# Attention and gated feed-forward on one core: softmax weights normalised on GpSimd before their transposes, and the weights' check moved into their decoding

## The chip, the cores and the metric

The kernel runs on one core of a Trainium2 chip. Its engines are TensorE (PE), VectorE (DVE), ScalarE (ACT), GpSimd (POOL) and the queue of SyncE (SP) that issues loads. The metric is the device time of one execution in microseconds; less is better.

## The reference

Banded causal attention with 8 global keys feeds a gated feed-forward block. B = 4, H = 8, S = 768, D = 64, d_model = 512, d_ff = 1024.

```python
scores = q @ k.T / sqrt(D) + bias            # bias: -slope * distance
keep   = (key < n_global) | ((rel >= 0) & (rel < n_local))     # 8 and 96
a = exp(where(keep, scores, -1e9) - max)
a = a / (a.sum(-1) + 1e-9)
x = a @ v                                    # heads side by side: B, S, 512
h = relu(x @ w_in)                           # B, S, 1024
c = conv over the sequence, 3 taps, per channel
out = (h * sigmoid(c)) @ w_out
```

The three feed-forward weights come as 64-bit floats.

## The kernel before

**Attention.** A job m is one batch, one half of the sequence (384 queries) and one pair of heads: 4 x 2 x 4 = 32 jobs. Each job has three steps of 128 queries, so there are 96 steps s. A step needs only 232 keys (136 in the first block of a sequence): 96 before, 128 own, 8 global. The parts of a step, by function:
- `scores`: TensorE, two heads into one PSUM tile `s` (two of these).
- `maxima`: VectorE adds the bias table and takes the row's least (`mm`).
- `exps`: ScalarE writes the exponentials to `pbuf[s % 3]` and their row sums to `sums`.
- `transposes`, LAG_T = 2 steps later: four TensorE transposes into PSUM `t`, copied by ScalarE to a tile `pt` (three of these).
- `values`, after a job's last step and LAG_V = 3 steps behind: PV, 24 matmuls into the one PSUM tile `pv`.

The exponentials go through the transposes and PV unnormalised. The inverse sums take a way of their own: `inverses` (VectorE, a sum and a reciprocal of 6 columns per job), `spread` (GpSimd copies them 64 times side by side into `wide`), `turned` (three TensorE transposes into `rt`, ScalarE copy to `rs`). `mixed` multiplies `pv` by `rs` on VectorE, GpSimd rounds it to `xh`, and VectorE leaves the rest in `xl`; products with high and low halves keep the precision.

**Feed-forward.** Four jobs make a unit of 384 rows, and there are 8 units. `mm1` (tile `h`, 96 matmuls a unit) and `relu`; `conv` (GpSimd takes the first tap, VectorE two more); `gate` (tanh on ScalarE); `split` (VectorE and ScalarE); `mm2` (tile `o`, 24 matmuls for each of 24 blocks of rows). This work is queued and `fill` puts it between the steps.

**Weights.** Sixteen pieces of 0.5 MB (`wr`) are decoded: three bit operations on VectorE (`weight_bits`), a cast on GpSimd (`weight_high`) and a subtraction on VectorE (`weight_low`). They are chores that `work` hands out from step 1 on with a budget per step. The fast path holds only for words of moderate size, so `check_weights` loads all 16 pieces again at the end (`check`) and VectorE takes each piece's smallest square, ScalarE the sum of squares. What is found goes into `bad`; one matmul (`total`) sums it over the partitions, and the flag decides whether the exact path `general` runs. With these inputs it does not.

**Order.** Steps 0 to 10 stand in the order in which the code is written (`manual_schedule`). From step 11 a scheduler with its own model of the engines sets the order on each engine; at run time each engine takes its instructions in that order and waits where an operand is missing.

Of the kernel before, what the change touches and what calls it, by code (L numbers as in the profile page):

```python
# [34 lines left out]
LAG_T, LAG_V = 2, 3  # L35
# [27 lines left out]
def fast_path(tc, io):  # L63
# [89 lines left out]
    reli = p2.tile([P, NT], I32, tag="pt", name="reli", bufs=NB)  # L153
# [14 lines left out]
    keyi = p2.tile([P, 64], I32, tag="pt", name="keyi", bufs=NB)  # L168
# [44 lines left out]
    misc = const.tile([P, 2 * NCHK + NLOW + 12], F32, name="misc")  # L213
# [3 lines left out]
    bad, ones, ebias, gbias = (rest[:, k : k + 1] for k in range(8, 12))  # L217
    G.memset(gbias, -0.96)

# [86 lines left out]
    words = []  # L306

    def check_loads(n):
        while len(words) < n:
            k = len(words)  # L310
            X = p1 if k % 3 == 2 else p2
            t = X.tile([P, HW, 2], I32, tag="rk" if k % 3 == 2 else "kk", name=f"check{k}")
            nc.sync.dma_start(t, weight_words(*divmod(k, 2)))
            words.append(t[:, :, 1].bitcast(F32))

    def check_weights():
        for k in range(NCHK):
            check_loads(k + 1)
            x = words[k]
            junk = p2.tile([P, HW], F32, tag="qh", name=f"junk{k}")  # L320
            j2 = p2.tile([P, HW], F32, tag="ql", name=f"junkb{k}")
            V.tensor_tensor_reduce(
                out=junk, in0=x, in1=x, scale=-1.0, scalar=-3.0e38,
                op0=ALU.mult, op1=ALU.max, accum_out=chk[:, k : k + 1],
            )
            A.activation(j2, x, AF.Square, accum_out=chk[:, NCHK + k : NCHK + k + 1])
        small, large = chk[:, :NCHK], chk[:, NCHK:]
        V.tensor_scalar(small, small, -1.5 * 2.0**-30, None, ALU.is_gt)
# [13 lines left out]
    st_s, st_pt, pv, xt, sums, rs, wides = {}, {}, {}, {}, {}, {}, {}  # L342
# [32 lines left out]
    def maxima(s):  # L375
        m, i = steps[s]
        b, u, hp = jobs[m]
        sp, c0, n, first = st_s[s]
        mm = p1.tile([P, 2], F32, tag="mm", name=f"mm{s}", bufs=6)
        if i == 0:  # L380
            sums[m] = p1.tile([P, 3, NB, 2], F32, tag="sums", name=f"sums{m}", bufs=3)
        for j in range(2):
            h = 2 * hp + j
            tb = tab[:, h, WIN:] if first else tab[:, h, 0:WIN]
            last_ttr[s] = V.tensor_tensor_reduce(  # L385
                out=sp[j][:, c0 : c0 + n], in0=sp[j][:, c0 : c0 + n], in1=tb,
                scale=-0.125, scalar=3.0e38, op0=ALU.add, op1=ALU.min,
                accum_out=mm[:, j : j + 1],
            )
        st_s[s] = (sp, c0, n, mm)  # L390

    def exps(s):
        m, i = steps[s]
        sp, c0, n, mm = st_s[s]
        pb = pbuf[s % NPB]
        for j in range(2):
            last_exp[s] = A.activation(  # L397
                pb[:, j, c0 : c0 + n], sp[j][:, c0 : c0 + n], AF.Exp,
                bias=mm[:, j : j + 1], scale=-1.0, accum_out=sums[m][:, 0, i, j : j + 1],
            )  # L400
        st_s[s] = (pb, c0)

    def inverses(m):
        su, more, inv = (sums[m][:, k] for k in range(3))
        V.tensor_scalar(more, su, 1.0e-9, None, ALU.add)
        V.reciprocal(inv, more)

    def spread(m):
        inv = sums.pop(m)[:, 2]
        wide = p2.tile([P, NB, 2, D], F32, tag="wide", name=f"wide{m}", bufs=1)  # L410
        G.tensor_copy(wide, inv.unsqueeze(3).broadcast_to([P, NB, 2, D]))
        wides[m] = wide.rearrange("p i j d -> p i (j d)")

    def turned(m):
        wide = wides.pop(m)
        pt = ps_t.tile([P, 2, 2, P], F32, tag="t", name=f"rt{m}")
        flat = pt.rearrange("p j c q -> p (j c q)")[:, :TB]
        for i in range(NB):
            T.transpose(flat[:, i * P : (i + 1) * P], wide[:, i], ident)  # L419
        rs[m] = p2.tile([P, TB], F32, tag="rs", name=f"rs{m}", bufs=1)  # L420
        A.activation(rs[m], flat, AF.Copy)

    def transposes(s):
        m, i = steps[s]
        pb, c0 = st_s.pop(s)
# [5 lines left out]
        sb = p2.tile([P, 2, 2, P], F32, tag="pt", name=f"pt{s}", bufs=NB)  # L431
# [7 lines left out]
    def values(m):  # L439
        pv[m] = ps_v.tile([P, TB], F32, tag="v", name=f"pv{m}")  # L440
        for i in range(NB):
            sb, ka = st_pt.pop(NB * m + i)
            for c, n in ((0, ka), (1, P - 24)):
                for j in range(2):
                    T.matmul(  # L445
                        pv[m][64 * j : 64 * j + 64, i * P : (i + 1) * P],
                        vt[m][:n, i, c, 64 * j : 64 * j + 64],
                        sb[:n, j, c, :],
                        start=c == 0,
                        stop=c == 1,  # L450
                    )

    def mixed(m):
        xh = px.tile([P, TB], F32R, tag="xh", name=f"xh{m}")
        xl = px.tile([P, TB], F32R, tag="xl", name=f"xl{m}")
        xt[m] = (xh, xl)
        x = rs.pop(m)
        V.tensor_tensor(x, pv[m], x, ALU.mult)  # L458
        G.tensor_copy(xh, x)  # L459
        cur["mixed"] = V.tensor_tensor(xl, x, xh.bitcast(F32), ALU.subtract)  # L460
# [215 lines left out]
    chores = {"dve": [], "pool": []}  # L676
# [12 lines left out]
    def piece_bits(i, half, n):  # L689
        weight_bits(i, half, n)  # L690
        if n == 2:
            chores["pool"].append((cur["s"], 0.7, piece_high, (i, half)))
            free_slot((i, half))
# [30 lines left out]
    for s in range(len(steps) + LAG_V + 1):  # L724
        cur["s"] = s
        m, i = steps[s] if s < len(steps) else (len(jobs), -1)
        if s < HAND:
            scores(s)
            if ends(s - LAG_V):
                values((s - LAG_V) // NB)  # L730
                turned((s - LAG_V) // NB)
            if s >= LAG_T:
                transposes(s - LAG_T)
            maxima(s)
# [20 lines left out]
            work("pool", 1.3)  # L755
        else:
            if hand:
                hand = False
                manual.__exit__(None, None, None)
# [15 lines left out]
            if s <= len(steps) and i < 1:  # L775
                inverses((s - 1) // NB)
                spread((s - 1) // NB)
# [4 lines left out]
            if ends(s - LAG_V):  # L782
                values((s - LAG_V) // NB)
                turned((s - LAG_V) // NB)
# [203 lines left out]
```

## Time and profile before

| | |
|---|---|
| median of 3 runs | 495.19 us (494.72 to 497.38) |
| the profiled execution | 490.68 us, span 488.8 us |
| busy in the span | TensorE 462.9 us, VectorE 364.7, ScalarE 287.3, GpSimd 164.9 |
| granted TensorE clock | mean 0.966 |

The profiled execution took 4.51 us less than the median of the runs, so a sum made against the profile is carried over to the runs as a difference. A busy TensorE is no proof that it bounds: its ends are modelled and overlap. The chain of waits and the idle time ahead of an instruction say more.

### The profile page before, as it was taken

Reading aid. Unit: us, or ns where it says so; the run is one execution under the profiler, and the core shown is the slowest. Engines: PE = TensorE matmul, PEld = TensorE weight load, DVE = VectorE, ACT = ScalarE, POOL = GpSimd, SP = SyncE. Lnnn points to the kernel's source line nnn. Section 1 sums busy time; section 2 is a strip of 40 time slices with the busy share of each in tenths; the row PEclk is TensorE's granted clock in tenths of the full one; section 3 lists DMA queues with packets and bytes.
Section 4 is the critical chain, followed back from the end, with each engine's and each line's share of the span. In section 5 each row is a group of like instructions: output and inputs, shape, how many; then the busy total and the mean of one; then the engine's idle time right before and its main releaser. Section 6 shows DMA issues by size and latency. Waiting matters only on the chain.

```text
span 488.8 us, 8824 instructions
## 1 busy us (share of the span) xinstructions
PE 462.9 (95%) x3109; PEld 398.1 (81%) x3109; DVE 364.7 (75%) x872; ACT 287.3 (59%) x774; POOL 164.9 (34%) x222
## 2 busy tenths in 40 slices
PE   7978999969999999999999999999999999999980
PEld 6855788759988998889888988899989988898860
DVE  4798879979999886857797887758797866167332
ACT  2543546667577585646785567557775774255542
POOL 4333344642553643323542542233434410020000
PEclk8898699998999999999999999999999999999996
DMA  7888662223332522343344323423342312100793
GB/s 191 217 210 255 200 174 89 78 91 107 92 113 98 163 68 87 121 142 108 108 129 130 101 66 115 138 87 101 127 129 96 100 57 84 44 0 23 252 302 119
DMA packets 21364, 60.01 MB, mean 123 GB/s; under 512 B 2880, under 2 KB 3136, under 8 KB 21312
## 3 DMA queue, kind: packets, MB, share of 16 engines
q1 hardware_dynamic: 17856, 53.21, 35.8%
q10 hardware_dynamic: 3456, 6.16, 3.4%
q8 instruction: 26, 0.43, 0.4%
q14 instruction: 26, 0.21, 0.1%
HBM read 53.07 MB, written 6.29 MB: 121 GB/s over the span
## 4 chain that ended last, share of the span: by engine, by line
PE 74%; DVE 14%; DMA 6%; issue 2%; ACT 2%; POOL 0%; SPq 0%; DVEq 0%; ACTq 0%; POOLq 0%
PE h L478 24%; PE o L589 21%; PE pv L445 9%; PE s L366 5%; DMA check<-in_w 5%; PE s L356 4%; PE t L429 4%; PE t L430 3%; PE rt L419 3%; DVE s L385 2%; DVE gl L580 1%; DVE c L577 1%; DVE c L526 1%; DVE c L525 1%; DMA rq<-in_qk 1%
## 5 line engine op out<-in xcount | busy, mean ns | idle before, releaser
L397 ACT ACTIVATE pbuf<-s,mm 128x232 f32<-128x232 f32 (+1 forms) x192 | 82.8, 437 | 73.8 <-DVE mm L385 71.9
L385 DVE CUSTOM_DVE_ANT_0 s<-s,tab 128x232 f32<-128x232 f32 (+1 forms) x192 | 73.8, 385 | 48.8 <-PE s L366 36.3
L524 POOL TENSOR_SCALAR c<-hbuf,cw 128x382 f32<-128x382 f32 (+1 forms) x64 | 47.3, 742 | 96.2 <-ACT hbuf L488 91.0
L589 PE MATMUL o<-woh,gh 128*128 128x512 f32 x192 | 78.5, 409 | 0.0
L589 PE MATMUL o<-wol,gh 128*128 128x512 f32 x192 | 76.2, 397 | 0.0
L589 PE MATMUL o<-woh,gl 128*128 128x512 f32 x192 | 76.1, 397 | 0.0
L445 PE MATMUL pv<-pt,v 104*64 104x128 f32 (+2 forms) x768 | 58.2, 289 | 4.0 <-DVE rs L458 2.9
L478 PE MATMUL h<-xh,wih 128*128 128x384 f32 x252 | 59.9, 348 | 0.0
L445 PEld LDWEIGHTS pv<-pt,v 104*64 104x64 f32 (+2 forms) x768 | 43.3, 141 | 19.6 <-issue 8.9
L525 DVE SCALAR_TENSOR_TENSOR c<-hbuf,cw,c 128x382 f32<-128x382 f32 (+1 forms) x64 | 44.9, 712 | 18.9 <-POOL c L524 18.8
L478 PE MATMUL h<-xl,wih 128*128 128x384 f32 x252 | 58.5, 346 | 0.1
L436 ACT ACTIVATE pt<-t 128x512 f32<-128x512 f32 x80 | 47.1, 599 | 18.5 <-PE t L430 18.2
L478 PE MATMUL h<-xh,wil 128*128 128x384 f32 x252 | 55.8, 342 | 0.0
L429 PE MATMUL t<-ident,pbuf 128*128 128x128 f32 (+1 forms) x192 | 48.9, 281 | 2.6 <-ACT pbuf L397 1.2
L488 ACT ACTIVATE hbuf<-h 128x384 f32<-128x384 f32 x64 | 31.2, 492 | 33.1 <-PE h L478 27.8
L430 PE MATMUL t<-ident,pbuf 128*128 128x128 f32 x192 | 48.3, 278 | 0.0
L459 POOL CAST xh<-rs 128x384 fp32r<-128x384 f32 x32 | 23.8, 743 | 65.6 <-DVE rs L458 65.4
L478 PEld LDWEIGHTS h<-xl,wih 128*128 128x128 f32 x252 | 43.5, 189 | 1.8 <-issue 1.5
L478 PEld LDWEIGHTS h<-xh,wil 128*128 128x128 f32 x252 | 44.3, 188 | 0.8 <-issue 0.8
L526 DVE SCALAR_TENSOR_TENSOR c<-hbuf,cw,c 128x382 f32<-128x382 f32 (+1 forms) x64 | 44.0, 701 | 0.8
L478 PEld LDWEIGHTS h<-xh,wih 128*128 128x128 f32 x252 | 43.5, 189 | 1.1 <-issue 0.8
L589 PEld LDWEIGHTS o<-woh,gl 128*128 128x128 f32 x192 | 36.1, 188 | 8.3
(110 smaller groups left out, 896.5 us busy)
## 6 DMA issues: line engine op xcount, KB each, us to landing
v<-in_vv SPq DMA_DIRECT2D x32, 384.0 KB, 3.1
rq<-in_qk SPq DMA_DIRECT2D x23, 384.0 KB, 3.3
wr<-in_w SPq DMA_DIRECT2D x16, 512.0 KB, 5.3
check<-in_w SPq DMA_DIRECT2D x16, 512.0 KB, 4.8
rk<-in_qk SPq DMA_DIRECT2D x12, 504.0 KB, 3.6
out<-ob ACTq DMA_DIRECT2D x23, 256.0 KB, 3.0
rk<-in_qk SPq DMA_DIRECT2D x11, 408.0 KB, 3.1
rq<-in_qk SPq DMA_DIRECT2D x9, 192.0 KB, 5.7
```

What stands on the lines that cost most here:

```text
L385: last_ttr[s] = V.tensor_tensor_reduce(out=sp[j][:, c0 : c0 + n], in0=sp[j][:, c0 : c0 + n], in1=tb, scale=-0.125, scalar=3.0e38, op0=ALU. ...
L397: last_exp[s] = A.activation(pb[:, j, c0 : c0 + n], sp[j][:, c0 : c0 + n], AF.Exp, bias=mm[:, j : j + 1], scale=-1.0, accum_out=sums[m][:, ...
L429: T.transpose(pt[:ka, j, 0, :], pb[:, j, c0:P], ident)
L430: T.transpose(pt[:, j, 1, :], pb[:, j, P:256], ident)
L436: last_ev[s] = A.activation(sb, pt, AF.Copy)
L445: T.matmul(pv[m][64 * j : 64 * j + 64, i * P : (i + 1) * P], vt[m][:n, i, c, 64 * j : 64 * j + 64], sb[:n, j, c, :], start=c == 0, stop=c ...
L478: T.matmul(ps[:, :TB], w_[:, k, fs], x_, start=part == 0 and k == 0, stop=part == 2 and k == NK - 1,)
L488: A.activation(half, ps[:, :TB], AF.Relu, scale=0.5)
L524: G.tensor_scalar(c, *tap(1), 1.0, ALU.mult, ALU.mult)
L525: V.scalar_tensor_tensor(c, *tap(0), c, ALU.mult, ALU.add)
L526: V.scalar_tensor_tensor(c, *tap(2), c, ALU.mult, ALU.add)
L589: T.matmul(ps, g_[:, f], w_[:, f], start=f == 0 and part == 0, stop=f == NF - 1 and part == 2,)
```

## The change

- `inverses` becomes `normalise`, once a step instead of once a job: VectorE adds 1e-9 to two sums and takes two reciprocals, and GpSimd multiplies the exponentials in `pbuf` by them in place, one instruction per head. It comes one step after `exps` and one before `transposes`. `spread`, `turned`, `wide`, `rt` and `rs` are gone.
- `mixed` is a ScalarE copy of `pv` to `xh` and a VectorE subtraction from `pv`.
- LAG_V is 4, there are four `pt` tiles, and the 24 PV matmuls of a job stand together, the last block first.
- The second load of the weights is gone. As a piece is decoded, ScalarE squares its words and sums them, then takes a relu of those squares with a bias and sums again: two instructions a piece, handed out as chores of their own (`act`), one in a step by hand. Both keep to one tile with the tag `ob`. The last five small VectorE operations of the check stay.

```diff
-LAG_T, LAG_V = 2, 3
+LAG_T, LAG_V = 2, 4
...
-    def check_weights():
-        for k in range(NCHK):
-            check_loads(k + 1)
-            x = words[k]
...
-            V.tensor_tensor_reduce(
-                out=junk, in0=x, in1=x, scale=-1.0, scalar=-3.0e38,
-                op0=ALU.mult, op1=ALU.max, accum_out=chk[:, k : k + 1],
-            )
-            A.activation(j2, x, AF.Square, accum_out=chk[:, NCHK + k : NCHK + k + 1])
+    def piece_check(i, half, n):
+        k = 2 * i + half
+        if n == 0:
+            squares[k] = p1.tile([P, HW], F32, tag="ob", name=f"square{k}")
+            x = wraw[i, half][:, :, 1].bitcast(F32)
+            A.activation(squares[k], x, AF.Square, accum_out=chk[:, NCHK + k : NCHK + k + 1])
+        else:
+            y = squares[k]
+            A.activation(
+                y, y, AF.Relu, bias=least, scale=-(2.0**30), accum_out=chk[:, k : k + 1]
+            )
...
-    def inverses(m):
-        su, more, inv = (sums[m][:, k] for k in range(3))
-        V.tensor_scalar(more, su, 1.0e-9, None, ALU.add)
-        V.reciprocal(inv, more)
...
-        G.tensor_copy(wide, inv.unsqueeze(3).broadcast_to([P, NB, 2, D]))
...
-        for i in range(NB):
-            T.transpose(flat[:, i * P : (i + 1) * P], wide[:, i], ident)
-        rs[m] = p2.tile([P, TB], F32, tag="rs", name=f"rs{m}", bufs=1)
-        A.activation(rs[m], flat, AF.Copy)
+    def normalise(s):
+        pb, c0, n, mm = st_s[s]
+        V.tensor_scalar(mm[:, 4:6], mm[:, 2:4], 1.0e-9, None, ALU.add)
+        V.reciprocal(mm[:, 6:8], mm[:, 4:6])
+        for j in range(2):
+            x = pb[:, j, c0 : c0 + n]
+            G.tensor_scalar(x, x, mm[:, 6 + j : 7 + j], 1.0, ALU.mult, ALU.mult)
...
     def values(m):
         pv[m] = ps_v.tile([P, TB], F32, tag="v", name=f"pv{m}")
-        for i in range(NB):
...
+        with contextlib.ExitStack() as es:
+            if "auto" in cur:
+                es.enter_context(tc.high_priority())
+                es.enter_context(tc.manual_schedule(engines={mybir.EngineType.PE}))
+            for i in (NB - 1, *range(NB - 1)):
+                block(m, i)
...
-        x = rs.pop(m)
-        V.tensor_tensor(x, pv[m], x, ALU.mult)
-        G.tensor_copy(xh, x)
-        cur["mixed"] = V.tensor_tensor(xl, x, xh.bitcast(F32), ALU.subtract)
+        A.activation(xh, pv[m], AF.Copy)
+        cur["mixed"] = V.tensor_tensor(xl, pv[m], xh.bitcast(F32), ALU.subtract)
...
-    with tc.issue_after(cur["mixed"].ins):
-        check_loads(3)
     last_tiles()
-    with tc.issue_after(cur["gated"].ins):
-        check_weights()
+    assert not any(chores.values())
+    check_weights()
```

How the instructions stand, at three places. First TensorE around the PV of job 22, in the long middle part. A row is line, operation, output <- inputs and size of one; `o` belongs to the feed-forward, `t` to the next step's transposes. Before:

```order
L589 MATMUL o_3_3533<-woh,gh_3_3009 128x512
L589 MATMUL o_3_3533<-wol,gh_3_3009 128x512
L589 MATMUL o_3_3533<-woh,gl_3_3010 128x512
L445 MATMUL pv_3578<-pt_3444,v_3350 64x128 x4
L445 MATMUL pv_3578<-pt_3500,v_3350 64x128 x4
L445 MATMUL pv_3578<-pt_3547,v_3350 64x128 x4
L419 MATMUL rt_3591<-ident,wide_3484 128x128 x3
L429 MATMUL t_3597<-ident,pbuf_191 128x128
```

Now:

```order
L575 MATMUL o_3_3677<-woh,gh_3_3145 128x512
L575 MATMUL o_3_3677<-wol,gh_3_3145 128x512
L575 MATMUL o_3_3677<-woh,gl_3_3146 128x512
L433 MATMUL pv_3722<-pt_3645,v_3428 64x128 x4
L433 MATMUL pv_3722<-pt_3520,v_3428 64x128 x4
L433 MATMUL pv_3722<-pt_3582,v_3428 64x128 x4
L575 MATMUL o_3_3677<-woh,gh_3_3145 128x512
L575 MATMUL o_3_3677<-wol,gh_3_3145 128x512
```

The three `rt` transposes are gone and feed-forward work follows PV at once.

Second, GpSimd, in the middle part too. Before, jobs 18 to 20: the taps `c`, the casts `qh` and `kk` of the next jobs' queries and keys, and for each job one `wide` and one `xh`.

```order
L524 TENSOR_SCALAR c_2616<-hbuf,cw 128x386 x2
L126 CAST qh_3014<-rq_2918 128x768
L125 CAST kk_3016<-rk_2917 128x1008
L411 COPY wide_2988<-sums_2831 128x384
L459 CAST xh_2981<-rs_2952 128x384
L126 CAST qh_3160<-rq_3054 128x768
L125 CAST kk_3162<-rk_3053 128x1008
```

Now, steps 49 to 53: two multiplications a step, with the casts in between.

```order
L126 CAST qh_2631<-rq_2536 128x768
L125 CAST kk_2633<-rk_2535 128x816
L402 TENSOR_SCALAR pbuf_193<-pbuf_193,mm_2502 128x232 x2
L402 TENSOR_SCALAR pbuf_194<-pbuf_194,mm_2544 128x232 x2
L402 TENSOR_SCALAR pbuf_192<-pbuf_192,mm_2581 128x136 x2
L402 TENSOR_SCALAR pbuf_193<-pbuf_193,mm_2645 128x232 x2
L126 CAST qh_2787<-rq_2681 128x768
```

`wide` and `xh` have left the engine; the multiplications of a step can stand behind two casts.

Third, the end of VectorE's program. Before: the copy of the last block's second half, the last two pieces of the check, its small operations and the flag (`misc` <- `total`).

```order
L599 COPY oc_5_5298<-o_5_5271 128x256
L322 ISA junk_5382,misc<-check_5380 128x512
L322 ISA misc 128x1
L322 ISA junk_5388,misc<-check_5386 128x512
L322 ISA misc 128x1
L329 TENSOR_SCALAR misc<-misc 128x16
L328 TENSOR_SCALAR misc<-misc 128x16
L330 TENSOR_SCALAR misc<-misc 128x16
L331 TENSOR_REDUCE misc<-misc 128x1
L332 TENSOR_TENSOR misc<-misc 128x1
L338 TENSOR_TENSOR misc<-misc 128x1
L825 TENSOR_SCALAR misc<-total 1x1
```

Now:

```order
L331 TENSOR_SCALAR misc<-misc 128x32
L332 TENSOR_REDUCE misc<-misc 128x1
L333 TENSOR_TENSOR misc<-misc 128x1
L566 TENSOR_TENSOR gl_5_5316<-hbuf,gh_5_5315 128x1024
L811 TENSOR_SCALAR misc<-total 1x1
L585 COPY oc_5_5431<-o_5_5404 128x256
```

All that `total` needs now stands ahead of the last block's operand `gl`, and the flag ahead of the last copy.

More of the change, by code (lines that the diff above doesn't have):

```diff
@@ L216, in fast_path @@
     odd, red, flag = rest[:, 0:3], rest[:, 3:7], rest[:, 7:8].bitcast(I32)
-    bad, ones, ebias, gbias = (rest[:, k : k + 1] for k in range(8, 12))
+    bad, ones, ebias, gbias, least = (rest[:, k : k + 1] for k in range(8, 13))
     G.memset(gbias, -0.96)
+    G.memset(least, 1.5)
     def limits():
@@ L304, in weight_low @@
         V.tensor_tensor(l[:, sl], t, h[:, sl].bitcast(F32), ALU.subtract)
[L306 to L314, printed above, removed]
-    def check_weights():
-        for k in range(NCHK):
-            check_loads(k + 1)
-            x = words[k]
-            junk = p2.tile([P, HW], F32, tag="qh", name=f"junk{k}")
-            j2 = p2.tile([P, HW], F32, tag="ql", name=f"junkb{k}")
-            V.tensor_tensor_reduce(
-                out=junk, in0=x, in1=x, scale=-1.0, scalar=-3.0e38,
-                op0=ALU.mult, op1=ALU.max, accum_out=chk[:, k : k + 1],
-            )
-            A.activation(j2, x, AF.Square, accum_out=chk[:, NCHK + k : NCHK + k + 1])
+    def piece_check(i, half, n):
[9 more added lines that the diff above has]
+            )
+    squares = {}
+    def check_weights():
         small, large = chk[:, :NCHK], chk[:, NCHK:]
-        V.tensor_scalar(small, small, -1.5 * 2.0**-30, None, ALU.is_gt)
+        V.tensor_scalar(small, small, 0.0, None, ALU.is_gt)
         V.tensor_scalar(large, large, 2.0**30, None, ALU.is_le)
@@ L341, in fast_path @@
     last_ttr = {}
-    st_s, st_pt, pv, xt, sums, rs, wides = {}, {}, {}, {}, {}, {}, {}
+    st_s, st_pt, pv, xt = {}, {}, {}, {}
     def scores(s):
@@ L440, in values, with block @@
         pv[m] = ps_v.tile([P, TB], F32, tag="v", name=f"pv{m}")
-        for i in range(NB):
[L442 to L451, printed above, removed]
+        with contextlib.ExitStack() as es:
[4 more added lines that the diff above has]
+                block(m, i)
+    def block(m, i):
+        sb, ka = st_pt.pop(NB * m + i)
+        for c, n in ((0, ka), (1, P - 24)):
+            for j in range(2):
+                T.matmul(
+                    pv[m][64 * j : 64 * j + 64, i * P : (i + 1) * P],
+                    vt[m][:n, i, c, 64 * j : 64 * j + 64],
+                    sb[:n, j, c, :],
+                    start=c == 0,
+                    stop=c == 1,
+                )
     def mixed(m):
@@ L690, in piece_bits @@
         weight_bits(i, half, n)
+        if n == 0:
+            for k in range(2):
+                chores["act"].append((cur["s"], 0.9, piece_check, (i, half, k)))
         if n == 2:
@@ L774, in fast_path @@
                 mixed(e // NB)
-            if s <= len(steps) and i < 1:
-                inverses((s - 1) // NB)
-                spread((s - 1) // NB)
+            if s <= len(steps):
+                normalise(s - 1)
             if s < LAG_V + SPU:
```

38 lines of the change are left out of this document (14 added, 24 removed).

## The prediction, made before the changed kernel was run

> **What bounds the kernel now.** I read the chain of waits by stages first, then the busy time of the same stages, then the end in order of time. The first three rows are the chain from 46 to 100 us, from 100 to 163 and from 163 to 452.3; the next three are busy time and count of each engine, granted clock, DMA share and GB/s.
>
> ```profile
> by line: PE h L478 32.4%; PE s L356 28.1%; PE pv L445 17.9%; PE t L429 6.5%; PE t L430 6.0%; PE rt L419 4.1%; PE h L499 4.0%; PE s L366 1.1%; issue 0.1%
> by line: DVE gl L580 11.5%; DVE c L577 10.6%; DVE s L385 9.8%; DVE c L526 9.7%; issue 9.0%; DVE c L525 8.6%; DVE ql L130 6.1%; PE pv L445 4.8%; DVE kk L129 4.3%; DVE xl L460 4.1%; DVE rs L458 3.8%; DVE mm L385 3.4%; ACT pbuf L397 3.3%; PE s
> by line: PE o L589 35.1%; PE h L478 34.0%; PE pv L445 10.6%; PE s L366 8.3%; PE t L430 4.3%; PE t L429 4.3%; PE rt L419 3.4%; issue 0.1%; ACT gh L579 0.0%
> ...
> 46.00:100.00 54.00, 53.95 (x339) 41.86 (x338) 47.41 (x129) 30.53 (x93) 24.85 (x30) 0.91 0.47 144
> 100.00:163.00 63.00, 58.56 (x409) 51.33 (x407) 58.38 (x120) 42.21 (x111) 26.25 (x29) 0.95 0.35 110
> 163.00:452.00 289.00, 289.00 (x1952) 255.71 (x1953) 212.00 (x480) 180.09 (x466) 96.95 (x120) 1.00 0.30 95
> ```
>
> From 163 to 452 us the chain is TensorE alone, at full clock: it waits for nobody, so an instruction taken from it there is time gained. Before that VectorE sets the pace, wholly from 100 to 163 us (58.38 of 63 us busy). The end is a third stage (start, duration, what):
>
> ```profile
> span 488.8 us, 8824 instructions
> ...
> 474.54 0.40 PE L589 MATMUL o<-woh,gl 128*128 128x512 f32 x1
> 482.37 0.19 PE L824 MATMUL total<-misc 128*1 128x1 f32 x2 [7.43 <-DVE misc L338]
> 482.60 0.15 DVE L825 TENSOR_SCALAR misc<-total 1x1 int32<-1x1 f32 x1 [0.37 <-PE total L824]
> ...
> 475.02 5.38 DMA check<-in_w
> 480.54 0.69 DVE junk L322
> ...
> check<-in_w SPq DMA_DIRECT2D x16, 512.0 KB, 4.8
> ```
>
> TensorE has done the last block at 474.94, then waits 7.43 us for the check, whose last load alone takes 5.38 us. The sums below go against this execution's 490.68 us; the median of the runs stands 4.51 us above it, and I carry the difference over.
>
> **The end.** No load is left after the last block, and the order puts all that `total` needs ahead of it. So `total` follows the last `o`: minus 7.4 us. Next in line is the last output, a ScalarE copy and a transfer:
>
> ```profile
> 478.39 0.37 ACT L597 ACTIVATE ob<-o 128x256 f32<-128x256 f32 x1
> out<-ob ACTq DMA_DIRECT2D x23, 256.0 KB, 3.0
> ```
>
> Some 0.37 + 0.4 + 3.0 = 3.8 us after the last matmul, against 482.75 to 488.8 = 6.05 us that follow the flag today; it stays inside. The worst case is half the gain, -3.7.
>
> **TensorE in the middle.** The `rt` transposes go: 3.4% of 289.3 us is 9.8 us. By single pieces, 20 groups (jobs 12 to 31) of the 0.48 us below give 9.6.
>
> ```profile
> 401.42 0.44 PE s L366 x4
> ...
> 417.45 0.48 PE rt L419 x3
> ...
> 405.87 0.20 ACT L397 ACTIVATION_READ_ACCUMULATOR pbuf<-s,mm 128x1 f32 x1
> 411.69 0.11 PE t L429
> ```
>
> PV itself is neither shorter nor longer, and at step 42 both orders have put out the same number of `s`, `t`, `pv`, `h` and `o` matmuls, so a later PV costs nothing there. What the gain hangs on is the new piece between the exponentials and their transposes: a sum, a reciprocal, two GpSimd multiplications. Their prices:
>
> ```profile
> L405 DVE TENSOR_SCALAR sums<-sums 128x6 f32<-128x6 f32 x32 | 6.7, 209 | 4.8 <-ACT pbuf L397 4.3
> L406 DVE RECIPROCAL sums<-sums 128x6 f32<-128x6 f32 x32 | 5.9, 186 | 0.5
> L198 POOL TENSOR_SCALAR keep<-loc 128x232 f32<-128x232 f32 x1 | 0.4, 387 | 5.9 <-DVE loc L197 5.9
> L580 DVE TENSOR_TENSOR gl<-c,gh 128x1024 fp32r<-128x1024 f32 x17 | 22.8, 1345 | 1.6 <-ACT gh L579 1.5
> L125 POOL CAST kk<-rk 128x1008 fp32r<-128x1008 f32 x12 | 15.5, 1295 | 2.5 <-DMA rk<-in_qk 2.4
> L126 POOL CAST qh<-rq 128x768 fp32r<-128x768 f32 x23 | 23.8, 1034 | 51.3 <-PE s L366 49.0 <-DMA rq<-in_qk 2.3
> L411 POOL COPY wide<-sums 128x384 f32<-128x384 f32 x32 | 23.6, 737 | 28.9 <-DVE sums L406 20.4 <-PE s L366 3.4 <-PE rt L419 3.0
> L459 POOL CAST xh<-rs 128x384 fp32r<-128x384 f32 x32 | 23.8, 743 | 65.6 <-DVE rs L458 65.4
> ```
>
> 0.209 + 0.186 + 2 x 0.387 = 1.2 us if all engines are free. If VectorE is at its longest operation (1.345) and both casts stand ahead on GpSimd (1.295 + 1.034), 4.8. The last step before (exponentials over at 406.07, first transpose at 411.69) had 5.6 us in between, and the 54 steps from 163 us to the last scores at 401.42 last 4.4 us each, with nearly two of them in between. The wait is covered: 0. GpSimd has room: 192 multiplications of 0.39 to 0.5 us are 69 to 87 us (narrow ones scaled by width), and 47.4 us of `wide` and `xh` go; 97 of 289 us were busy. ScalarE trades one 384-wide copy from PSUM (`rs`) for another (`xh`): 0.
>
> **The front, up to 163 us.** Here VectorE counts. Rows still missing:
>
> ```profile
> L458 DVE TENSOR_TENSOR rs<-pv,rs 128x384 f32<-128x384 f32 x32 | 17.5, 548 | 9.7 <-ACT rs L421 9.3
> L460 DVE TENSOR_TENSOR xl<-rs,xh 128x384 fp32r<-128x384 f32 x32 | 20.6, 645 | 1.3 <-POOL xh L459 1.2
> L326 ACT ACTIVATE junkb<-check 128x512 f32<-128x512 f32 x16 | 10.8, 674 | 12.9 <-DMA check<-in_w 12.0 <-ACT ob L603 0.8
> L326 ACT ACTIVATION_READ_ACCUMULATOR junkb<-check 128x1 f32 x16 | 3.1, 192 | 0.0
> ...
> 108.11 3.02 PE L445 MATMUL pv<-pt,v 32*64 32x128 f32 x24 [2.92 <-DVE rs L458]
> 108.12 1.17 POOL L459 CAST xh<-rs 128x384 fp32r<-128x384 f32 x1 [6.29 <-DVE rs L458]
> 409.21 0.51 POOL L459 CAST xh<-rs 128x384 fp32r<-128x384 f32 x1 [13.16 <-DVE rs L458]
> 81.01 0.61 DVE L526 SCALAR_TENSOR_TENSOR c<-hbuf,cw,c 128x382 f32<-128x382 f32 x1
> 109.73 1.10 DVE L526 SCALAR_TENSOR_TENSOR c<-hbuf,cw,c 128x382 f32<-128x382 f32 x1
> ```
>
> - VectorE, per job: three pairs of 0.395 come, one pair and `rs` (0.548) go, and `xl` reads PSUM as `rs` did, 0.548 for 0.645: +0.145 us, +2.0 for 14 jobs.
> - `add` waits for the exponentials: 4.3 us in 32 times, 0.134 each. 42 in place of 14 are +3.8; about half of the front is VectorE's: +1.9.
> - The check's five small operations now stand at steps 32 to 34: 5 x 0.17, +0.9.
> - GpSimd beside VectorE: `xh` took 0.51 alone and 1.17 beside it, and VectorE's tap 0.61 alone and 1.10 beside it, 0.49 lost to 1.17 of GpSimd, or 0.42 per us. GpSimd gets 14 x (6 x 0.45 - 1.48) = 17 us more here. If half of it meets such an operation, 3.6; if only the 63 us that are wholly VectorE's count, 1.4. I take +2.0.
> - ScalarE gets 32 x 0.87 = 28 us of check instead of 14 at the end. The order spreads it over steps 1 to 31, where ScalarE is 57% busy (30.53 of 54), and has done before its fullest part: 0, at worst inside the bounds below.
> - A weight's slot is free only after the square; with 4 slots, and squares at most two steps behind the bits, the loads on SP's queue and those behind them still come in time: 0.
> - Gains: `rt` in TensorE's own stretch, 4.1% of 54 us, -2.2. And PV of job 8 waited 2.92 us for `rs`, which no longer exists; VectorE idled about half of that: -1.5.
>
> Together +2.0 + 1.9 + 0.9 + 2.0 - 2.2 - 1.5 = +3.1. Bounds: only the gains, -3.7; all prices in full and no gain, 2.0 + 3.8 + 0.9 + 3.6 = +10.3.
>
> [...]
>
> **The sum.** -7.4 - 9.8 + 3.1 = -14.1 us: 490.68 becomes 476.6, and 495.19 becomes 481.1 us for the runs. With the front at its ends, -20.9 to -6.9: 474.3 to 488.3.
>
> **The rivals.**
> 1. TensorE starves, and the kernel is slower. The transposes stand in a queue on which all else waits behind them; if GpSimd's multiplications come later than the scheduler thought, every step waits. The 4.8 us above stay under 5.6, so it needs more than the worst queue shown. It decides at (17.2 - 3.1) / 54 = 0.26 us a step in the middle; at 0.5 us a step, 27 us, the runs take 495.19 - 14.1 + 27 = 508. For it: GpSimd is the least predictable engine here (0.51 or 1.17 for one form). Against: TensorE waited for nothing in 289 us. Such waits would also cost clock, since PV took 3.02 us after the wait at 108 and 1.47 elsewhere (row below). 7%.
> 2. VectorE is slowed by GpSimd in the front at the full price: 488 us. In the middle it could not bind: 212 us plus 19 x 0.145, plus 23 x 0.42, are 224 of 279. 10%.
> 3. The change does not shorten the middle, because what looks like TensorE's pace is the pace of the steps (scores, maxima, exponentials in two `s` tiles): only the end's gain, 495.19 - 7.4 + 3.1 = 491 us. Against: no wait of TensorE there. 6%.
>
> ```profile
> 97.73 1.47 PE pv L445 x24
> ```
>
> [...]
>
> **How the numbers follow.** The likeliest case has 77%, the rivals 7, 10 and 6. About 0.5% (2.5 us) is what the measurement tells from no change. The second and third rival still end faster; the first spreads over unchanged and slower, with half a part of the unknown. Faster 0.88, same 0.05, slower 0.07. The range takes in the front's bounds and the second rival: 474 to 489 us.
>
> **What would show it.** Right: no `rt`; TensorE without waits after step 42 and at clock 1.00; `total` within 1 us of the last `o`; the stage up to step 42 about 3 us longer; VectorE's mean of the taps (L525, L526 before) up by some hundredths. Wrong: `t` waiting for GpSimd's `pbuf` in the middle, a granted clock below 1.00 there, or `total` still waiting.

## The result, and the profile after

| | before | changed |
|---|---|---|
| median of the timed runs, first timing | 495.53 us (4 runs) | 477.66 us (4 runs) |
| ratio of the two, 95% interval | | 0.969 (0.963 to 0.975) |
| median, second timing (the last experiment) | 492.87 us (11 runs) | 478.75 us (6 runs) |
| ratio of the two, 95% interval | | 0.972 (0.966 to 0.978) |
| the profiled execution, first timing | 490.68 us, span 488.8 | 476.23 us, span 474.4 |

The changed kernel is 17.9 us faster by the medians of the first timing, 14.1 us by those of the second and 14.45 us by the two profiled executions. The forecast was minus 14.1 us and 481.1 us. Executions of one kernel differ here by up to 16 us (488.2 to 504.0 us in 50 runs of the kernel before), and most of the section on the experiments turns on why. Ratios and their intervals leave out executions more than 1.5% above the fastest of their kernel; medians are over all.

First the chain of waits of the changed kernel, from 100 to 163 us and from 163 to 452.3, then the busy time of the stages (columns as before: TensorE, its weight loads, VectorE, ScalarE, GpSimd, granted clock, DMA share, GB/s).

```profile
by line: PE h L464 10.4%; DVE c L511 9.9%; issue 8.9%; DVE c L512 8.8%; DVE c L563 7.8%; DVE gl L566 7.3%; DVE s L378 7.2%; DVE kk L129 6.7%; DVE ql L130 5.3%; ACT pbuf L390 4.4%; PE pv L433 3.5%; DVE mm L398 3.0%; ACT pt L417 2.5%; PE s L3
by line: PE o L575 36.9%; PE h L464 33.3%; PE pv L433 10.5%; PE s L361 8.5%; PE t L410 4.5%; PE t L411 4.3%; DVE gl L566 0.8%; DVE kk L129 0.6%; POOL pbuf L402 0.4%; DVE s L378 0.3%; issue 0.2%; DVE mm L378 0.0%; DVE xl L446 0.0%; DVE mm L3
...
46.00:100.00 54.00, 53.05 (x321) 41.21 (x321) 48.78 (x142) 40.92 (x124) 32.16 (x48) 0.87 0.52 160
100.00:163.00 63.00, 56.14 (x392) 48.38 (x390) 54.54 (x136) 44.64 (x122) 41.22 (x48) 0.95 0.31 99
163.00:452.00 289.00, 288.58 (x1949) 255.53 (x1948) 216.59 (x537) 179.80 (x471) 154.51 (x195) 1.00 0.28 92
```

`rt` is gone from the middle. TensorE still is the chain there at clock 1.00, and the new link, GpSimd's `pbuf`, holds 0.4% of it. GpSimd's busy time rose from 96.95 to 154.51 us without TensorE noticing. From 100 to 163 us VectorE now is busy for 54.54 us where it was for 58.38, though it got more to do; TensorE idles more (56.14 for 58.56).

Then the end, in order of time:

```profile
435.25 32.70 PE o L575 x144
467.94 0.02 issue
467.96 0.39 ACT ob L583
468.36 0.02 issue
468.38 0.42 DVE oc L585
...
467.54 0.39 PE L575 MATMUL o<-woh,gl 128*128 128x512 f32 x1
467.86 0.19 PE L810 MATMUL total<-misc 128*1 128x1 f32 x2
```

The last `o` ends at 467.93 (before: 474.94) and `total` follows at once; 6.47 us of output and flag remain, where 13.86 us followed the last `o` before. I split each span at two marks, the start of step 42's exponentials and the end of the last `o`:

| | up to step 42 | to the last `o` | end | span |
|---|---|---|---|---|
| before | 172.89 | 302.05 | 13.86 | 488.8 |
| changed, first timing | 173.96 | 293.97 | 6.47 | 474.4 |
| difference | +1.1 | -8.1 | -7.4 | -14.4 |
| forecast | +3.1 | -9.8 | -7.4 | -14.1 |
| changed, second timing | 180.47 | 293.99 | 6.44 | 480.9 |

The last row is the same program as the second: middle and end are alike to 0.03 us, and the front is 6.5 us longer.

### The profile page after: what moved, and what is told of

Its sections match the earlier page's. It is cut to its first block, busy times and chain, and to the rows that moved or that the text cites. A ratio compares the mean times of both kernels' runs of the same rounds, so it can differ in the third digit from the quotient of the medians.

```text
span 474.4 us, 8982 instructions
## 1 busy us (share of the span) xinstructions
PE 453.7 (96%) x3013; PEld 388.4 (82%) x3013; DVE 355.9 (75%) x936; ACT 293.4 (62%) x806; POOL 250.1 (53%) x351
## 4 chain that ended last, share of the span: by engine, by line
PE 77%; DVE 15%; ACT 2%; issue 2%; POOL 1%; DMA 1%; SPq 0%; POOLq 0%; DVEq 0%; ACTq 0%
PE o L575 26%; PE h L464 25%; PE pv L433 9%; PE s L361 5%; PE s L351 4%; PE t L410 4%; PE t L411 3%; DVE s L378 2%; DVE gl L566 1%; DVE c L511 1%; ACT pbuf L390 1%; DVE c L512 1%; DVE c L563 1%; DMA rq<-in_qk 1%; POOL pbuf L402 1%
## 5 line engine op out<-in xcount | busy, mean ns | idle before, releaser
L402 POOL TENSOR_SCALAR pbuf<-pbuf,mm 128x232 f32<-128x232 f32 (+1 forms) x192 | 137.6, 728 | 88.6 <-DVE mm L399 60.7
L575 PE MATMUL o<-woh,gh 128*128 128x512 f32 x192 | 77.4, 403 | 0.0
L464 PE MATMUL h<-xh,wil 128*128 128x384 f32 x252 | 57.9, 343 | 0.0
L410 PE MATMUL t<-ident,pbuf 128*128 128x128 f32 (+1 forms) x192 | 51.3, 286 | 3.9 <-POOL pbuf L402 3.3
L411 PE MATMUL t<-ident,pbuf 128*128 128x128 f32 x192 | 50.4, 281 | 0.0
## 6 DMA issues: line engine op xcount, KB each, us to landing
rk<-in_qk SPq DMA_DIRECT2D x12, 504.0 KB, 3.5
```

The lines of the kernel that those rows point to most:

```text
L402: G.tensor_scalar(x, x, mm[:, 6 + j : 7 + j], 1.0, ALU.mult, ALU.mult)
L410: T.transpose(pt[:ka, j, 0, :], pb[:, j, c0:P], ident)
L411: T.transpose(pt[:, j, 1, :], pb[:, j, P:256], ident)
L464: T.matmul(ps[:, :TB], w_[:, k, fs], x_, start=part == 0 and k == 0, stop=part == 2 and k == NK - 1,)
L575: T.matmul(ps, g_[:, f], w_[:, f], start=f == 0 and part == 0, stop=f == NF - 1 and part == 2,)
```

## The experiments

**Each part alone.** The kernel without any check of the weights, in both orders, goes with these two and completes a table.

The changed kernel with the old check at the end:

```diff
-                chores["act"].append((cur["s"], 0.9, piece_check, (i, half, k)))
...
+    with tc.issue_after(cur["mixed"].ins):
+        check_loads(3)
     last_tiles()
+    with tc.issue_after(cur["gated"].ins):
+        check_weights()          # second load, VectorE reduce and ScalarE square of 16 pieces
```

> The changed kernel with the old check of the weights (a second load of all 16 pieces at the end), all else as changed. My theory, three separate terms: the end is worth 7.4 us and ScalarE's share of the check costs nothing in the front, so the span goes from 474.4 to about 482 us and `total` again waits some 7 us after the last `o`. Rival: the check on ScalarE is what made the front 3 us longer; then the front gets its 3 us back and the span is about 479 us.

The kernel before with only the new check, the same edit the other way round:

> The kernel before with only the check moved into the decoding. My theory: the same 7.4 us from the other side, span 488.8 - 7.4 = 481.4 us, TensorE's waits and the front as before. Rival: the longer ScalarE programme in the front costs 2 to 3 us, span 484 us. A second rival: the runs of before stand 4.5 us above its profiled execution because the loads of the old check vary from run to run; then the time of the runs falls by more than the span, to 484 us or less in place of 488.

The changed kernel and the kernel before with no check at all (the flags are set by one memset):

```diff
+    G.memset(chk, -1.0)
...
-                chores["act"].append((cur["s"], 0.9, piece_check, (i, half, k)))
```

> The changed kernel without any check of the weights (neither on ScalarE nor at the end; the flags are set to passing values). Theory A, each piece has its own price: the check's 32 ScalarE operations (28 us, all before step 42) cost the front what they cost when they were put alone into the kernel before, about 7 us, so the last o ends near 461 us instead of 467.9 and the time is near 470 us. Theory B, the front's length is set by how the order falls out (waits between ScalarE, VectorE and GpSimd) and not by the amount of work: the last o ends near 475 us, as in the run with the old check at the end, and the time is near 485 us, slower than the changed kernel though it does less.

> The kernel before without any check of the weights. Theory A: only the end's wait goes: the last o stays near 475 us, the span is 481.4 and the time 487.5 us, 4 us under the run with the check on ScalarE. Theory B: the front moves by several microseconds although nothing that stands in it is touched: last o outside of 472 to 478 us.

Ratios to the kernel before on the same chip, with intervals, and medians:

| | check at the end | check on ScalarE | no check |
|---|---|---|---|
| inverse sums turned by TensorE | 1 (493.0 us) | 0.998 (0.994 to 1.002), 491.6 us | 0.981 (0.975 to 0.988), 485.3 us |
| exponentials normalised | 1.000 (0.996 to 1.003), 493.2 us | 0.969 and 0.972, 478.2 us | 0.977 (0.974 to 0.981), 482.6 us |

Neither part alone is worth anything that can be measured, and both together 3%. My terms gave a span of 481 to 482 us for each alone; the median spans are 491.4 and 489.2, so both expectations missed, the rivals' too. And with no check at all the changed kernel is not faster than with it: its median is some 4 us higher, on another chip and with intervals that overlap (theory A of that run missed; B gave the last `o` at 475, where it is at 475.35, though the next run offers another reason than B's). For the kernel before without a check, theory A's 487.5 us is 2 us above the median; the one execution with a trace, the slowest of its four, has the last `o` at 481.09, as theory B says. The middle and the end of these runs do what they should: the new check alone ends 6.6 us after the last `o` instead of 13.86, and there the last `o` is 7.4 us later than before. The front eats it.

**The same program twice.** How much the front varies without any change shows in the last run, the changed kernel once more:

> The changed kernel itself once more, beside the kernel before on the chip of this study. Three variants of it that do the same work or less (no add, no check, more idle matmuls) took 482.6 to 483.9 us, 5 to 6 us more than the 477.7 us of the changed kernel, which was timed elsewhere. Theory E (the scheduler's order of the front, which is another in each variant, makes the 5 to 6 us): 476 to 480 us here too, ratio to the kernel before 0.965 to 0.975. Rival F (the four runs of the changed kernel were lucky in chip or clock, and all four variants are alike): 481 to 485 us, ratio 0.98 to 0.99.

It took 478.75 us in the median, inside theory E's range, but with two of six runs at 482.8 us, as slow as the variants that do the same or less; so it doesn't show that their order of the front made them slower. The profiled execution is one of those two. The same stretches in both executions of this program, first timing and then second:

```profile
45.00:60.00 15.00, 15.00 (x64) 10.21 (x64) 12.73 (x39) 11.87 (x39) 6.21 (x11) 0.54 0.85 255
60.00:73.00 13.00, 13.00 (x98) 10.52 (x96) 10.49 (x32) 8.79 (x28) 7.70 (x14) 1.00 0.39 108
73.00:80.00 7.00, 7.00 (x55) 5.81 (x54) 7.00 (x21) 4.93 (x15) 2.72 (x5) 1.00 0.34 111
...
45.00:60.00 15.00, 14.91 (x58) 10.11 (x60) 12.42 (x39) 11.56 (x38) 5.92 (x11) 0.52 0.89 251
60.00:73.00 13.00, 13.00 (x54) 10.23 (x53) 6.91 (x22) 4.71 (x17) 4.86 (x9) 0.50 0.37 112
73.00:80.00 7.00, 7.00 (x57) 5.50 (x55) 4.74 (x13) 4.65 (x13) 3.73 (x6) 1.00 0.13 38
```

Both times TensorE falls to half clock at 45 us. The first time the full clock is back by 60 us, the second time only near 73. In between TensorE is "busy" 13.00 of 13 us in both, but has done 54 matmuls instead of 98. In slices of 2 us, the time at half clock up to 163 us is 37.5 us in the first and 51.1 us in the second, 13.6 us more, and the last `o` comes 6.53 us later: 0.48 us per microsecond at half clock. Over the 50 runs of the kernel before, a hundredth less of mean clock goes with 3.7 us more (correlation 0.93), which is 0.38 us per microsecond at half clock (a hundredth of 490 us is 9.8 us at half clock); over the 40 of them that the ratios use it is 2.8 us (correlation 0.75), or 0.29. So most of the spread of the kernel before goes with its clock. It isn't all: the four runs of the changed kernel's first timing have 476.23 us at 0.959 and 478.19 at 0.966.

That also reads the other kernels. Half-clock time up to 163 us, the last `o`, and the latter less 0.48 us per microsecond of the former:

| kernel (profiled execution) | half clock | last `o` | less 0.48 x |
|---|---|---|---|
| changed, first timing | 37.5 | 467.93 | 449.9 |
| changed, second timing | 51.1 | 474.46 | 449.9 |
| changed, old check | 78.5 | 487.10 | 449.4 |
| changed, no check | 51.2 | 475.35 | 450.8 |
| changed, no add (below) | 51.2 | 474.17 | 449.6 |
| before | 23.8 | 474.94 | 463.5 |
| before, new check | 27.2 | 482.30 | 469.2 |
| before, no check | 44.3 | 481.09 | 459.8 |

The slope comes from the first two rows alone, and puts three other normalising kernels, whose last `o` lies up to 19 us later, within 1 us of them. It does not do so for every variant: the two below that give TensorE more to do (idle transposes, the old place of PV) have 37.5 and 34.1 us at half clock, no more than the first row, and their last `o` comes 13.7 and 13.9 us later. With the old check in the changed kernel, the execution with a trace ran its front twice as long at half clock. This row of it, against the changed kernel of the first timing behind it, shows it:

```profile
0.00:80.00 80.00, 74.96 (x371) 55.80 (x372) 50.03 (x169) 25.37 (x90) 28.83 (x74) 0.55 0.62 171
...
0.00:80.00 80.00, 73.83 (x488) 56.21 (x489) 64.61 (x209) 50.42 (x161) 37.95 (x88) 0.81 0.66 186
```

That execution took 504.35 us, 11 more than the median of its kernel, so the medians must decide: 493.2 us at a mean clock of 0.941 with the old check, 478.2 at 0.957 without. Of these 15 us the end is 7.4, and the clock, at 2.8 to 3.7 us a hundredth, 4.5 to 6; some 2 to 3 us stay open. By the same table ScalarE's check costs the changed kernel nothing that can be told (449.9 with it, 450.8 without), as forecast. In the kernel before it costs, by this reckoning, 5.7 us that are not clock, and the medians agree: 1.4 us were gained where the end gives 7.2, at a mean clock no lower (0.967 for 0.961). TensorE is busy there for 68.28 us of the first 80 where it was for 72.24, and ScalarE for 48.38 instead of 37.17:

```profile
0.00:80.00 80.00, 72.24 (x515) 56.94 (x516) 62.91 (x188) 37.17 (x123) 28.94 (x61) 0.89 0.71 200
...
0.00:80.00 80.00, 68.28 (x490) 53.36 (x492) 61.87 (x183) 48.38 (x156) 27.93 (x60) 0.87 0.65 183
```

Why it costs in the one order and not in the other was not settled. That the kernel before without a check comes out 3.7 us under the one with it, although nothing in its front was touched but a memset, shows what this reckoning can tell: the lower rows are good to some 4 us.

**Is it the clock?** More and fewer of the idle matmuls that follow each of the steps ordered by hand:

```diff
-WARM = (43, 0, 16, 16, 16, 12, 8, 4, 4, 4, 4, 4)
+WARM = (43, 0, 16, 16, 16, 16, 16, 16, 16, 16, 16, 16)     # more
+WARM = (43, 0, 8, 8, 8, 4)                                 # fewer
```

> The changed kernel with more idle TensorE matmuls on zeros in the hand-ordered front: WARM gives 16 behind each of steps 1 to 10 where it gave 16, 16, 16, 12, 8, 4, 4, 4, 4, 4. Theory C (what differs between kernels and between runs of one kernel in the front is how long TensorE runs at half clock, and that follows gaps in its work): the half-clock time in the first 80 us, 29 us in the changed kernel's profile, falls to 15 us or less, mean clock 0.970 or more, time 470 to 475 us by the 3.6 us that a hundredth of mean clock was worth in 30 runs of the kernel before. Rival D (the half-clock phases come as they come, or the front is VectorE's): clock stays 0.955 to 0.966, time 477 to 482 us, since 60 matmuls of 0.055 to 0.11 us come in between.

> The changed kernel with fewer of those idle matmuls (8, 8, 8, 4 and then none). Theory C: longer gaps, so the half-clock stretch reaches from 26 us or earlier to 70 us or later as in the runs without the check or with the old one, mean clock 0.95 or less, time 482 to 492 us. Rival D: clock as in the changed kernel, time 474 to 479 us, for the queue is 50 matmuls shorter.

That is 72 more and 60 fewer than the changed kernel's 88 (the expectations said 60 and 50). The scheduler put both into nearly one order behind step 10, another than the changed kernel's, so they are compared with each other. More: 483.8 us, 41 us at half clock. Fewer: 487.1 us, 78.5 us at half clock, 65 of them from 8 to 73 us without a break. The first 80 us of both:

```profile
0.00:80.00 80.00, 73.88 (x528) 57.28 (x529) 61.34 (x201) 47.15 (x154) 39.62 (x86) 0.83 0.68 181
...
0.00:80.00 80.00, 76.41 (x359) 56.54 (x361) 56.35 (x187) 42.85 (x141) 32.98 (x81) 0.59 0.63 176
```

So with 132 idle matmuls fewer the half clock lasted 37.5 us longer in these two executions: theory C met for fewer (time and stretch), though one of its four runs had a mean clock of 0.966 and took 484.6 us, 0.7 more than one at 0.931. For more it missed: the fall at 45 us came all the same, and the time was 2 us over the rival's range. The intervals of the two ratios, 0.976 to 0.990 and 0.981 to 0.997, overlap. The last `o` differs by only 6.6 us for 37.5 us of half clock, 0.18 us each, since the idle matmuls take queue time themselves (132 of them, each 0.055 to 0.11 us from its start to the next one's in the changed kernel's trace, are 7 to 15 us).

**The middle.** Three idle transposes per job put back:

```diff
+            flat = ps_t.tile([P, 2, 2, P], F32, tag="t", name=f"rt{m}")
...
+            for i in range(NB):
+                T.transpose(flat[:, i * P : (i + 1) * P], ident, ident)
```

> The changed kernel with three TensorE transposes of the identity after each job's PV, into the `t` buffers, that nobody reads: the TensorE work of the old `rt` alone. My theory: 20 groups of 0.48 us in the middle are 9.6 us, and some 2 us more in TensorE's own stretch of the front: span 484 to 486 us. Rival: the steps set the pace in the middle, and what went was the chain over `wide` and `rs`, not TensorE's time; then the span stays within 2 us of 474.4.

489.5 us, ratio 0.990 (0.987 to 0.994). From step 42 to the last `o` it took 299.42 us instead of 293.97, 5.4 us of the 8.1 that had been gained; the rest of its loss is front (step 42 at 182.17, 8.2 us later with the same 37.5 us at half clock, where 2 us were expected; why so much isn't shown). So the transposes do sit on TensorE's own time, which refutes the third rival.

The old place of PV, with three `pt` tiles and the scheduler free:

```diff
-LAG_T, LAG_V = 2, 4
+LAG_T, LAG_V = 2, 3
...
-            for i in (NB - 1, *range(NB - 1)):     # as one piece
+        for i in range(NB):                         # wherever the scheduler puts it
             block(m, i)
```

> The changed kernel with PV three steps behind, in plain order, placed by the scheduler, and three pt tiles, as before; normalising on GpSimd and the new check stay. My theory: the lag and the one piece are worth little by themselves: TensorE in the middle waits for pt tiles or transposes by under 0.1 us a step, under 5 us in all, so the stage from 163 to 452 us stays at clock 1.00 and the time is 477 to 483 us. Rival: the later PV is what covers the new chain (sum, reciprocal, multiplication, transpose, copy); without it each job waits about half a microsecond in TensorE's queue, 20 jobs, and the time is 488 us or more, as much as rt took.

491.2 us, ratio 0.997 (0.993 to 1.001): the whole gain gone, as the rival said, but not by its mechanism. From step 42 (181.88 us) to the last `o` (481.85) it took 299.97 us, 6.0 more than the changed kernel, and the other 7.9 us were lost in the front, at no more half-clock time. In the middle the waits hardly grew: from 163 to 452 us TensorE waits 0.9 us for GpSimd and 2.0 for VectorE's `xl`, and from 200 to 400 us not at all. What grew there is the work itself. The chain by line from step 42 to the last `o`, changed kernel first:

```profile
by line: PE o L575 41.6%; PE h L464 31.4%; PE pv L433 10.3%; PE s L361 8.2%; PE t L410 4.3%; PE t L411 4.2%
by line: PE o L571 41.1%; PE h L460 30.7%; PE pv L429 11.1%; PE s L361 7.8%; PE t L410 5.1%; PE t L411 4.2%
```

Both are TensorE alone. PV takes 11.1% of 299.97 us for 10.3% of 293.97, 3.0 us more, and the transposes 2.9 more: nearly all of the 6.0. The timeline says why. One piece of the changed kernel, then a split one:

```profile
310.83 1.54 PE L433 MATMUL pv<-pt,v 128*64 128x128 f32 x24
312.30 0.33 PE L361 MATMUL s<-kk,ql 128*128 128x136 f32 x1
...
309.27 1.10 PE L429 MATMUL pv<-pt,v 128*64 128x128 f32 x16
310.30 0.33 PE L410 MATMUL t<-ident,pbuf 128*128 128x128 f32 x1
310.46 0.27 PE L411 MATMUL t<-ident,pbuf 128*128 128x128 f32 x1
310.67 0.66 PE L429 MATMUL pv<-pt,v 128*64 128x128 f32 x8
311.26 0.33 PE L410 MATMUL t<-ident,pbuf 128*128 128x128 f32 x1
```

24 matmuls take 1.47 us to the next start, 0.49 per 8. The piece of 8 takes 0.59, starts 0.21 us after a transpose that is followed by its like after 0.11, and the transpose behind it needs 0.05 more than such a one: 0.25 us for each piece into which PV is cut. The trace has 45 pieces from step 42 on, and 19 in the changed kernel; 26 x 0.25 = 6.5 us, for the 6.0 measured. Lag, one piece and the fourth `pt` tile went back together here, and what the front's 7.9 us come from isn't shown.

**The normalising.** Left out (the exponentials go on as they are, so the gate's values leave the fast range and the exact path runs behind; only the part up to the last `o` is read), and its multiplications doubled:

```diff
+            G.tensor_scalar(x, x, 1.0, 1.0, ALU.mult, ALU.mult)     # doubled
```

> The changed kernel with nothing in place of the normalising: the sums are taken but no VectorE sum and reciprocal and no GpSimd multiplication (the output is not normalised). My theory: the middle is TensorE's alone and gains nothing, the front gets back the 3 us that normalising cost, span about 471 us. Rival: normalising also holds up the middle in small waits (TensorE waited for GpSimd in 18 places), then the span falls below 468 us.

> The changed kernel with a second GpSimd multiplication (by 1.0) behind each of the 192, so that GpSimd's part between exponentials and transposes is twice as long. My theory (5.6 us were there, the chain needs 1.2 to 4.8): the middle has little left once the multiplications take 0.7 us each as measured: 2 x 0.7 us a step come on top; GpSimd's busy time in the middle goes from 154.5 to about 245 of 289 us, TensorE waits for pbuf now and then, 0 to 0.2 us a step, time 478 to 492 us. The first rival of the prediction (TensorE starves): 0.5 us a step and more, 54 steps, the granted clock in the middle under 1.00, time above 505 us.

Without it the last `o` ends at 460.76, 7.2 us earlier, all of it in the front (step 42 at 164.57 instead of 173.96, of which the middle gives 2.2 us back); the theory's 3 us were too few, and the rival's gain in the middle isn't there. Doubled, the kernel takes 498.8 us, ratio 1.013 (1.004 to 1.021), between the two expectations; from step 42 to the last `o` 302.03 us, 8.1 more, or 0.15 us a step: TensorE starts to wait, but at clock 1.00.

```profile
163.00:452.00 289.00, 281.14 (x1941) 247.69 (x1940) 223.65 (x547) 181.86 (x484) 214.47 (x326) 1.00 0.33 99
...
PE s L361 <- ACT pbuf L390: 4.9, 4, 1.7
PE t L411 <- POOL pbuf L403: 2.3, 3, 1.8
```

(The second part is TensorE's waits in this stretch: total, times, longest; behind step 42, which comes at 190.78 us here, waits add up to 5.7 us.) So the middle has room for one dose of GpSimd and not for two.

Without the addition ahead of the reciprocal:

```diff
-        V.tensor_scalar(mm[:, 4:6], mm[:, 2:4], 1.0e-9, None, ALU.add)
-        V.reciprocal(mm[:, 6:8], mm[:, 4:6])
+        V.reciprocal(mm[:, 6:8], mm[:, 2:4])
```

> The changed kernel without the addition of 1e-9 ahead of the reciprocal (the sums are at least 1 here, so fp32 results are the same): 96 VectorE operations of 254 ns less, 24.4 us of busy time, 12 us of it in the front. Theory A (VectorE's work sets the front from 100 to 163 us): half of the front's 12 us is gained, 3 to 6 us, time 472 to 475 us; the wait for the exponentials moves to the reciprocal. Theory B (order, not work): within 3 us of the changed kernel, or slower.

483.9 us in the median of four, too scattered for a ratio: 474.1 us, inside theory A's range, and three from 482.7 to 485.9. At an equal mean clock of 0.945 the two kernels agree: 482.71 us here, 482.77 and 482.75 in the second timing. With 51.2 us at half clock each, step 42 comes 2.7 us earlier than there (177.76 for 180.47), but the middle takes it back, and the last `o` is at 474.17 for 474.46. The 474.1 us had a mean clock of 0.972, above all ten runs of the changed kernel (0.945 to 0.966), and 2.8 to 3.7 us a hundredth account for it. So 24 us of VectorE's time less bring nothing that these runs can tell, which is theory B.

## Why the prediction was right, and where it was not

- **The end**, -7.4: measured -7.4. `total` starts 0.07 us before the modelled end of the last `o`. Step right.
- **The middle**, -9.8 or 9.6: measured -8.1, at clock 1.00. Right in kind and sized a fifth too large: 20 groups of 0.48 us were counted. From step 42 on there are 19, and a group holds TensorE for less than 0.48, since that took in the modelled end of the last transpose. From the start of a group to the start of what follows it is 0.38 us where other transposes follow, as here in the kernel before:

```profile
222.09 0.55 PE L419 MATMUL rt<-ident,wide 128*128 128x128 f32 x3
222.47 0.27 PE L429 MATMUL t<-ident,pbuf 128*32 128x128 f32 x1
```

  and in all 7.5 us for the 19. The idle transposes, mostly followed by larger matmuls after 0.30 us, come to 6.1 by the same count, and 5.4 were measured.
- **The cover of the GpSimd chain**, 0: right. TensorE waits 0.2 us for `pbuf` from 163 to 452 us. The first rival's mechanism is real but needs a second dose.
- **"A later PV costs nothing"**: true, but it hid a term. With PV's old place, free of the one piece and with three `pt` tiles, the scheduler cuts PV into 45 pieces, which explains 6.0 us in the middle, and the front is 7.9 us longer: the change then brings nothing. The prediction counted this part as neutral; it is a condition of the gain.
- **ScalarE's check**, 0: right in this order (449.9 against 450.8), by a margin that the forecast could not know, as it costs 5.7 us in the order before.
- **The front**, +3.1: measured +1.1 in the first timing and +7.6 in the second, inside the bounds of -3.7 to +10.3, but not for the reasons given. That the whole came out at -14.4 in the profiled execution, for a forecast of -14.1, is luck in part: the middle gave 1.7 us less and the front cost 2.0 less. The step that the runs don't bear out is "Here VectorE counts". Taking 24 us of work from VectorE, some 12 of them in the front, gave nothing that could be told. The terms of the sum were VectorE's, and two of them were contention paid by VectorE (+2.0) and waits of `add` (+1.9). The profile of the changed kernel shows what they came to: first GpSimd's multiplications (count, minimum, median and maximum in ns), then their mean, VectorE's two taps, and VectorE's `add`, whose wait for the exponentials was 0.23 us each (22.4 in 96) and not 0.134.

```profile
L402 POOL TENSOR_SCALAR pbuf<-pbuf,mm x192: 372/459/2572, 10.8 to 402.2; 128x232 f32<-128x232 f32 x160, 128x136 f32<-128x136 f32 x32
...
L402 POOL TENSOR_SCALAR pbuf<-pbuf,mm 128x232 f32<-128x232 f32 (+1 forms) x192 | 137.6, 728 | 88.6 <-DVE mm L399 60.7 <-ACT pt L417 7.0 <-ACT pbuf L390 6.6
L512 DVE SCALAR_TENSOR_TENSOR c<-hbuf,cw,c 128x382 f32<-128x382 f32 (+1 forms) x64 | 45.3, 711 | 0.5
L511 DVE SCALAR_TENSOR_TENSOR c<-hbuf,cw,c 128x382 f32<-128x382 f32 (+1 forms) x64 | 43.8, 691 | 16.6 <-POOL c L510 16.3
L398 DVE TENSOR_SCALAR mm<-mm 128x2 f32<-128x2 f32 x96 | 24.4, 254 | 22.7 <-ACT pbuf L390 22.4
```

  The estimate of 0.39 to 0.5 us was right for the median (0.459) and not for the mean, 0.728, because some last up to 2.57 us, like this pair of 3.50 us beside four operations of VectorE with two inputs each. VectorE pays as well: behind them stand a tap of 1.18 us and an `add` of 0.98 beside a GpSimd cast (in each pair of views GpSimd's row first).

```profile
256.21 3.50 POOL L402 TENSOR_SCALAR pbuf<-pbuf,mm 128x232 f32<-128x232 f32 x2 [0.53 <-DVE mm L399]
...
255.96 0.96 DVE L130 TENSOR_TENSOR ql<-rq,qh 128x768 fp32r<-128x768 f32 x1
256.83 2.63 DVE L563 SCALAR_TENSOR_TENSOR c<-c,hbuf 128x16 f32<-128x16 f32 x3
...
140.14 1.35 POOL L125 CAST kk<-rk 128x1008 fp32r<-128x1008 f32 x1
...
139.44 1.18 DVE L512 SCALAR_TENSOR_TENSOR c<-hbuf,cw,c 128x386 f32<-128x386 f32 x1
140.53 0.98 DVE L398 TENSOR_SCALAR mm<-mm 128x2 f32<-128x2 f32 x1
```

  Over the whole trace of the changed kernel, VectorE's taps take 0.61 us in the mean where GpSimd is busy for under a tenth of them (55) and 0.80 where it is for over seven tenths (45); `add` takes 0.16 and 0.33 (41 and 52). The mean of the taps, 712 and 701 ns before and 691 and 711 now, did not rise as the prediction's sign would have it, because GpSimd was beside them before too (0.61 for 67 of them and 0.85 for 33). By an estimate that takes the shortest tenth of each form as its price alone, VectorE's operations up to step 42 hold 17.8 us of stretching before and 19.8 now, so as busy time the term of +2.0 came out, and the full price of 3.6 did not. GpSimd's hold 20.3 and 30.8 (the profile's own legend calls its spans rough). That such busy time is lost time in the front, no run shows. What the runs do price is the chain as a whole: at equal half-clock time normalising is worth 8.8 us (449.9 against 460.76 - 0.48 x 41.0 = 441.1), and a second dose on GpSimd 7 us in the front (465.0 - 449.9 less the 8.1 in the middle). As the second dose is GpSimd's alone, and taking `add` from VectorE brought nothing, the length of the chain over GpSimd is the likelier cost, rather than VectorE's work; that is argued, not shown.
- **What the front gained** was sized too small. At equal half-clock time step 42 comes at 172.89 - 11.4 = 161.5 before and 173.96 - 18.0 = 156.0 after, so 5.5 us earlier instead of 3.1 later (by the 0.29 of the kernel before, 2.9 earlier). Against a price of some 8 us for normalising, the gains of the front are then an estimated 11 to 14 us, and not 2.2 + 1.5. What they consist of isn't shown: besides the old way of the inverse sums, PV's place is a candidate, as the run with the old place lost 7.9 us in the front. The longer half-clock time (23.8 to 37.5 us, 6.6 us of time at 0.48) took most of it back. The prediction has no term for the clock of the front. The clock accounts for a good part of why normalising alone, with the old check, looked worthless; it does not for the new check alone, whose front lost 5.7 us to something else. Whether the new order itself invites longer half-clock stretches, or the executions drew them, ten runs do not tell.

## What to carry to other kernels

Before you compare two versions, look at the granted clock of both stage by stage, and at several executions of each: half-clock time that comes and goes (here 37.5 and 51.1 us in two executions of one program, whose last `o` lay 6.53 us apart) can hide a part of a real gain (here that of normalising with the old check) or show a false one. Price a new operation on an engine off the critical path at its mean beside the neighbours it will have, not at its time alone (here 0.728 us in the mean, for 0.39 to 0.5 estimated). And when a change frees the order in which a scheduler works, look at whether it cuts small matmuls of another shape into pieces: here 45 pieces of PV instead of 19 cost the middle about 6 us of a gain of 14.

## What the hardware showed that I had not expected

- The stretches at half clock in the front of these traces are whole multiples of about 3.4 us. By slices of 2 us they are, in the changed kernel's first timing, 6.8 us (within 8 to 16 us), 10.2 (28 to 40), 13.7 (44 to 60) and twice 3.4 (104 to 108 and 144 to 150); others are 20.5 us with more idle matmuls, 23.9 in the kernel before without a check, 37.6 without the addition and 44.4 without a check. In the second timing TensorE shows no gap over 0.2 us from 45.1 us on, and yet the half clock lasts until about 73 us, 27.3 us in all. Nor did a long idle time stand ahead of that fall: the gaps over 0.2 us in the 20 us before it were 1.1, 0.7, 0.6 and 0.4 us.
- Where GpSimd and VectorE work side by side in the changed kernel's trace, both are stretched: GpSimd's 128x232 multiplication takes 0.45 to 2.57 us, 0.46 in the mean where two-input operations of VectorE are beside it for under a twentieth of it and 0.98 where they are for over half; VectorE's taps go from 0.61 to 0.80 us and its `add` from 0.16 to 0.33.
